# Another order of steps for the end of an attention, routing and expert kernel on one core

## The chip, the core and the metric

One core of a Trainium2 chip runs the whole program. The metric is the device time of one execution in microseconds (us). TensorE (PE) multiplies, with weight loads (PEld) beside it; VectorE (DVE), ScalarE (ACT) and GpSimd (POOL) do the elementwise work; SyncE (SP) issues most transfers. Each engine takes its instructions in the order of the program, and waits on semaphores where a result or a buffer comes from elsewhere.

## What is computed

The reference is an attention, a mixture of eight experts and a second multiplication stage, one behind the other:

```python
# attention: 4 x 12 heads, 448 positions, 64 wide; q and k normalised per row, then
scores = scale * (q_n @ k_n.T);  attn = softmax(scores);  x = attn @ v
# x becomes 1792 tokens x 768; experts: D = 768, E = 8, F = 1024
logits = x @ w_gate;  expert_idx = argmax(logits);  gate_w = its softmax probability
out[mask] = gate_w[mask] * (max(x[mask] @ w1[e], 0) @ w2[e])      # for each expert e
# second stage, on the experts' output x
h = (x @ w1) * (x @ w2) @ w3
return h @ w_out
```

## The kernel before

**Stages.** The attention runs over 12 groups of heads (about 0 to 325 us). Beside it the kernel multiplies w3 by w_out once (called W here; TensorE line 264), so that the second stage needs one product less. Then the tokens are routed, the experts run one after the other (from 372.9 us, lines 940, 964 and 968), and the second stage follows.

**The order.** Every piece of work is a generator that yields steps, each for one engine. `ORDER` is a string of 1388 two-character codes; `Flow.run` takes them in turn, sends the next step of that piece and pins the order on every engine. Nothing reorders steps afterwards. So the table alone sets in what order each engine, SP's queue among them, comes to its instructions.

**W.** A 64-bit piece of w3 or w_out is loaded (line 215, tile `w64`, two buffers), turned to 32-bit numbers by three DVE instructions (lines 205 to 207), split into a high and a low half (ACT lines 227 and 228, then POOL or DVE line 231, tile `w3r`), and for w3 turned by a DMA transpose (line 237, tile `w3t`). For the later pieces of the w3 rows from row block 4 on, second column half, there is one `w3r` buffer, so ACT line 228 of one such piece waits until the transpose of the one before has landed. A block of W, (row block f, column half n), is 24 matmuls of 128x384 into one PSUM buffer (`psw` or `pswl`), written out by ACT line 267, DVE line 269 and a store on SP (line 271). The three `s` PSUM buffers are shared by `pswl` blocks, by `psx` below and by the attention's scores before.

**Routing.** `route` (lines 590 to 632) compares the gate's sums `lacc` (line 525), finds each token's expert, and counts ranks by matmuls (`psr`, lines 614 to 618). `slots` (lines 660 to 676) makes masks `mk`, multiplies (`psi`, line 673) and writes the row numbers `ix0` of the first expert. `gather` fetches that expert's rows by three indirect transfers on POOL (line 723, tile `xr`), turns them with 36 small matmuls (line 742, `psx`) and copies them (DVE line 746, ACT line 748); expert 0 starts on TensorE behind that. `offsets` (lines 761 to 792) computes all positions `qi`; 14 indirect stores on POOL write the sorted list `md` (line 536), from which SP reads the next expert's rows (line 719).

**First expert's weights.** `prefetch` loads six pieces of w1 (line 698, ACT line 701, DVE line 703) and `prefetch2` eight of w2 (line 708, ACT line 711, DVE line 713) through three buffers `pf`.

Below, the functions that the diff touches.

Of the kernel before, what the change touches and what calls it, by code (L numbers as in the profile page):

```python
# [1462 lines left out]
```

## Time and profile before

| what | us |
|---|---|
| three runs: lowest, median, highest | 955.47, 956.5, 957.8 |
| the profiled execution | 957.36 |
| its span in the profile | 955.6 |

Busy shares over that span are PE 91%, DVE 66%, ACT 52% and POOL 33%. The mean hides that different engines bound different stretches: DVE is nearly full up to 140 us, PE from there to 325 us, and from 325 to 373 us neither is. A row of the timeline gives the start, the busy time, the engine, the line, the operation, what it writes and reads, the shape and the count; brackets hold the idle time of that engine just before and what ended it. In the table of windows PEclk is the granted clock of TensorE, 1.00 being 2.4 GHz and 0.50 being 1.2 GHz, and the DMA column is the mean busy share of the 16 DMA engines.

### The profile page before, as it was taken

Reading aid. Unit: us, or ns where it says so; the run is one execution under the profiler, and the core shown is the slowest. Engines: PE = TensorE matmul, PEld = TensorE weight load, DVE = VectorE, ACT = ScalarE, POOL = GpSimd, SP = SyncE. Lnnn points to the kernel's source line nnn. Section 1 sums busy time; section 2 is a strip of 40 time slices with the busy share of each in tenths; the row PEclk is TensorE's granted clock in tenths of the full one; section 3 lists DMA queues with packets and bytes.
Section 4 is the critical chain, followed back from the end, with each engine's and each line's share of the span. In section 5 each row is a group of like instructions: output and inputs, shape, how many; then the busy total and the mean of one; then the engine's idle time right before and its main releaser. Section 6 shows DMA issues by size and latency. Waiting matters only on the chain.

```text
span 955.6 us, 19437 instructions
## 1 busy us (share of the span) xinstructions
PE 871.3 (91%) x7766; PEld 587.8 (62%) x7766; DVE 626.2 (66%) x924; ACT 492.5 (52%) x770; POOL 315.5 (33%) x325
## 2 busy tenths in 40 slices
PE   0588999999999979899899999999889999999996
PEld 0255666666666645577688999975444445456664
DVE  6998998878998765247356787999964755120000
ACT  4877888888977443144356666654333323110000
POOL 6367567766733113410010101001443534131111
PEclk9989999999999997899899999999999999999999
DMA  7868799787589993386679899820322211111111
GB/s 186 184 140 198 179 191 195 142 177 156 110 219 216 223 253 83 130 231 183 207 245 285 246 296 299 266 84 2 109 67 66 67 45 50 50 67 50 50 50 50
DMA packets 200351, 144.44 MB, mean 151 GB/s; under 512 B 139376, under 2 KB 178832, under 8 KB 200256
## 3 DMA queue, kind: packets, MB, share of 16 engines
q1 hardware_dynamic: 197248, 131.39, 53.7%
q0 software_dynamic: 3008, 11.76, 3.6%
q8 instruction: 63, 1.03, 0.4%
q14 instruction: 32, 0.26, 0.1%
HBM read 103.52 MB, written 14.18 MB: 123 GB/s over the span
## 4 chain that ended last, share of the span: by engine, by line
PE 41%; DVE 7%; issue 2%; DMA 1%; ACT 1%; SPq 1%; POOLq 0%; ACTq 0%
PE psm L940 30%; PE pso L1433 11%; DVE m2w L1182 1%; DVE y32w L207 1%; DVE y32w L206 1%; DVE y32w L205 1%; DMA st<-in_moe_w_dram 1%; DVE c L1354 1%; DVE c L1344 0%; DVE b L1053 0%; SPq L957 0%; DVE c L1346 0%; ACT b L1050 0%; DMA sx<-in_moe_w_dram 0%; DVE y L1067 0%
## 5 line engine op out<-in xcount | busy, mean ns | idle before, releaser
L940 PE MATMUL psm<-b,m2w 128*128 128x512 f16 (+1 forms) x1008 | 193.8, 355 | 9.7 <-DVE m2w L1182 6.8
L940 PEld LDWEIGHTS <-m2w 128*128 128x128 f16 x1008 | 98.9, 98 | 104.3 <-DVE m2w L1182 8.0
L940 PEld LDWEIGHTS <-w1t 128*128 128x128 f16 x1152 | 110.8, 100 | 28.6 <-issue 9.9
L940 PE MATMUL psm<-ht,w2t 128*128 128x320 f16 (+7 forms) x1152 | 124.4, 270 | 0.0
L940 PEld LDWEIGHTS <-w2t 128*128 128x128 f16 x1152 | 109.2, 98 | 14.1
L940 PE MATMUL psm<-xte,w1t 128*128 128x288 f16 (+6 forms) x1008 | 107.2, 269 | 6.6 <-DMA sx<-in_moe_w_dram 4.7
L1433 PE MATMUL pso<-ww,ab 128*128 128x384 f16 x672 | 109.4, 326 | 0.0
L404 DVE TENSOR_REDUCE nm<-psm 128x2 f32<-128x896 f32 x84 | 88.6, 1083 | 9.8 <-PE psm L402 9.4
L1433 PEld LDWEIGHTS <-ab 128*128 128x128 f16 x672 | 65.8, 98 | 43.6
L1325 POOL TENSOR_TENSOR ab<-c,ab 128x384 f16<-128x384 f32 (+1 forms) x32 | 39.1, 1233 | 155.4 <-ACT ab L1324 152.1
L461 PE MATMUL po<-vf,e 128*128 128x65 f32 (+1 forms) x576 | 88.8, 272 | 1.5 <-issue 1.5
L402 PE MATMUL psm<-kt,qt 64*64 64x448 f16 x336 | 48.9, 390 | 40.6 <-DMA qt<-qf 27.9
L461 PEld LDWEIGHTS po<-vf,e 128*128 128x128 f32 (+1 forms) x576 | 69.9, 177 | 16.6 <-issue 13.3
L723 POOL DMA_INDIRECT xr<-xd,ix x19 | 20.8, 1097 | 177.6 <-DMA ix<-md 116.7
L1130 DVE SCALAR_TENSOR_TENSOR w1t<-st,w1t 128x1024 f16<-128x1024 f32 x42 | 50.8, 1223 | 35.7 <-ACT w1t L1124 34.4
L1437 DVE TENSOR_SCALAR ob<-pso,meta_s 128x384 f32<-128x384 f32 x14 | 8.7, 618 | 99.1 <-PE pso L1433 99.1
L431 PE MATMUL pss<-qt,kt 64*128 64x448 f16 (+1 forms) x576 | 67.3, 375 | 5.1 <-DVE e L446 4.0
L464 PE MATMUL po<-v,e 128*128 128x65 f16 (+1 forms) x480 | 63.8, 195 | 1.7 <-DVE lacc L525 1.7
L465 PE MATMUL po<-vl,e 128*128 128x64 f16 (+1 forms) x480 | 63.8, 194 | 0.0
L466 PE MATMUL po<-v,e 128*128 128x65 f16 (+1 forms) x480 | 63.0, 194 | 0.0
L1324 ACT ACTIVATE ab<-c 128x384 f16<-128x384 f32 (+1 forms) x32 | 18.2, 576 | 81.7 <-DVE c L1354 72.7
L1436 ACT ACTIVATE ob<-pso,meta_s 128x384 f32<-128x384 f32 x14 | 8.1, 580 | 98.8 <-PE pso L1433 98.8
(247 smaller groups left out, 1700.4 us busy)
## 6 DMA issues: line engine op xcount, KB each, us to landing
st<-in_moe_w_dram SPq DMA_DIRECT2D x42, 512.0 KB
st<-in_moe_w_dram SPq DMA_DIRECT2D x44, 384.0 KB
st<-in_moe_w_dram SPq DMA_DIRECT2D x48, 256.0 KB
w<-in_moe_w_dram SPq DMA_DIRECT2D x16, 512.0 KB
w<-in_moe_w_out_dram SPq DMA_DIRECT2D x16, 384.0 KB
xd<-rx SPq DMA_DIRECT2D x12, 448.0 KB
kf<-in_k_dram SPq DMA_DIRECT2D x24, 192.0 KB
qf<-in_q_dram SPq DMA_DIRECT2D x24, 192.0 KB
```

Of the source, the lines that this page charges most:

```text
L402: nc.tensor.matmul(ps[h, z, 0:S], lhsT=s["q"][0][h, c:c + 64], rhs=s["k"][0][h, S * j:S * j + S], start=True, stop=True)
L404: nc.vector.tensor_reduce(s["nm"][:, t], ps[:, :, 0:S], axis=AX.X, op=ALU.max, negate=True)
L431: nc.tensor.matmul(ps[o, h, 0:S], lhsT=l, rhs=rt[HD[h], S * j:S * j + S], start=a == 0, stop=a == 3)
L461: nc.tensor.matmul(ov[r, t, :], lhsT=e[0], rhs=vfs[i % 2][:, h, c, 0:D + 1], start=z == 0, stop=z == 3)
L464: nc.tensor.matmul(ov[r, t, :], lhsT=e[0], rhs=vh, start=z == 0, stop=False)
L465: nc.tensor.matmul(ov[r, t, 0:D], lhsT=e[0], rhs=s["vl"][:, h, c, :], start=False, stop=False)
L466: nc.tensor.matmul(ov[r, t, :], lhsT=e[1], rhs=vh, start=False, stop=z == 3)
L723: nc.gpsimd.indirect_dma_start(out=dst, out_offset=None, in_=xd, in_offset=bass.IndirectOffsetOnAxis(ap=ix[0:dst.shape[0], t:t + 1], axis=0))
L940: nc.tensor.matmul(ps, lhsT=x, rhs=y, start=first and j == 0, stop=last and j == n - 1, **kw)
L1130: nc.vector.scalar_tensor_tensor(t[:, 1], st, 32.0, t[:, 0], op0=ALU.mult, op1=ALU.subtract)
L1325: nc.gpsimd.tensor_tensor(ab[f][:, 1, cs], x, ab[f][:, 0, cs], op=ALU.subtract)
L1433: nc.tensor.matmul(pp[z], lhsT=ab[f][:, x, ts], rhs=ww[f][:, y, z * 384:(z + 1) * 384], start=f == 0 and x == 0 and y == 0, stop=f == 7 an ...
```

## The change

Only `ORDER` differs: four strings near its start (steps of 40 to 92 us) and its last 185 steps (from about 322 us up to the start of expert 0). No instruction is added or taken out: each engine has as many rows as before.

```diff
@@ -46,10 +46,10 @@
-    "0o0k0s1b0o0E200s1d0A0E0w0J1N0Acw1a0q0w1c1a0i1c0m1c0q1a0K0i0m221+0u0C0qcs0OcAcw22cs2Ycs0u261+0y0C0ucE2U1e0ycA1m24cw1e241q"
+    "0o0k0s1b0o0E200s1d0A0E0w0J1N0Acw1a0q0w1c1a0i1c0m1c0q1a0K0i0m221+0u0C0qcs0OcA22cs2Ycs0u261+0y0C0ucw2UcE1e0ycA1m24cw1e241q"
...
@@ -65,10 +65,10 @@
-    "d2doc+8ubfd6bgbgbgakc+dobgdoc+dod2dodudobibgbgdodwd6bsdybAdwbGd6dydubCdydwbGdwbEdubCbOdyd2dqbEbIdqdqdqbsbsbKdodqc4dqd6dq"
+    "d2do8ubfbgbgc+bgakc+dobgdodobic+bgdodudobgbsdobAbGdubCbEdududubsbsc4bsdudmdodudsdsdsc4c4d6d6bGbIc6c6c6d6dsdsdsdsdsdudwdw"
...
```

**The end of the attention.** The first place is on DVE, from `route`'s last instruction (line 609) to the masks `mk` and the row numbers `ix0`; `w1t` and `w2t` are weights of the first expert, `wsp` is a finished block of W, `w32` a piece of w3 on its way into W. Before:

```order
L609 CAST ohs_147<-ohf_148 128x56
L703 SCALAR_TENSOR_TENSOR w1t_5359<-pf_4962,w1t_5359 128x1024
L703 SCALAR_TENSOR_TENSOR w1t_5368<-pf_4411,w1t_5368 128x1024
L703 SCALAR_TENSOR_TENSOR w1t_5380<-pf_4304,w1t_5380 128x1024
L621 COPY rank_150<-psr_5410 128x56
L623 TENSOR_REDUCE sums_149<-ohf_148 128x8
L663 TENSOR_TENSOR fa_5427<-ohf_148,foh_153 128x56
L664 SCALAR_TENSOR_TENSOR fa_5427<-rank_150,fa_5427 128x56
L665 TENSOR_REDUCE fv_5428<-fa_5427 128x7
L668 TENSOR_SCALAR mk_5432<-slot_144,fv_5428 128x384 x7
L713 SCALAR_TENSOR_TENSOR w2t_5448<-pf2_5386,w2t_5448 128x768
L625 TENSOR_TENSOR ex_5324<-lg_5322,mx_5323 128x56
```

After:

```order
L609 CAST ohs_147<-ohf_148 128x56
L269 SCALAR_TENSOR_TENSOR wsp_5303<-psw_5204,wsp_5303 128x384
L621 COPY rank_150<-psr_5355 128x56
L623 TENSOR_REDUCE sums_149<-ohf_148 128x8
L663 TENSOR_TENSOR fa_5366<-ohf_148,foh_153 128x56
L664 SCALAR_TENSOR_TENSOR fa_5366<-rank_150,fa_5366 128x56
L665 TENSOR_REDUCE fv_5367<-fa_5366 128x7
L668 TENSOR_SCALAR mk_5371<-slot_144,fv_5367 128x384 x7
L625 TENSOR_TENSOR ex_5308<-lg_5306,mx_5307 128x56
L676 TENSOR_TENSOR ix0_146<-psi_5398,part_145 128x3
L205 TENSOR_SCALAR w32_5421<-w64_5087 128x512
L206 SCALAR_TENSOR_TENSOR w32_5421<-w64_5087,w32_5421 128x512
```

Three `w1t` pieces no longer stand between lines 609 and 621, and a `w2t` piece, a block `wsp` and a `w1t` piece no longer stand between lines 668 and 676; they, and two conversions of w3 that stood around the last `lacc` (line 525), come behind line 676.

Still on DVE, later, from the last copies of the turned rows (`xt0`) to the start of `offsets` (line 764). Before:

```order
L713 SCALAR_TENSOR_TENSOR w2t_5640<-pf2_5577,w2t_5640 128x768
L746 CAST xt0_5591<-psx_5676 128x640
L764 COPY own_155<-eidx_140 128x8
L765 COPY own_155<-psc_5620 128x8
L768 SCALAR_TENSOR_TENSOR key_5721<-own_155,rev_141 128x8
L769 SCALAR_TENSOR_TENSOR key_5721<-foh_153,key_5721 128x8
L770 TENSOR_TENSOR more_5722<-key_5721 128x64
```

After:

```order
L746 CAST xt0_5518<-psx_5581 128x640
L703 SCALAR_TENSOR_TENSOR w1t_5619<-pf_5615,w1t_5619 128x1024
L703 SCALAR_TENSOR_TENSOR w1t_5622<-pf_5617,w1t_5622 128x1024
L713 SCALAR_TENSOR_TENSOR w2t_5631<-pf2_5629,w2t_5631 128x768
L764 COPY own_155<-eidx_140 128x8
L765 COPY own_155<-psc_5588 128x8
L768 SCALAR_TENSOR_TENSOR key_5704<-own_155,rev_141 128x8
L769 SCALAR_TENSOR_TENSOR key_5704<-foh_153,key_5704 128x8
```

Two `w1t` pieces and a `w2t` piece now stand ahead of `offsets`; each waits for its own load.

The second place is SP's queue over the last two turnings of w3 (line 237) and the first expert's weight loads (lines 698 and 708). Before:

```order
L237 DMA_TRANSPOSE w3t_5443<-w3r_5319 128x8x128
L698 ISA
L698 DMA pf_5469<-in_moe_w1_dram 128x1024
L708 ISA
L708 DMA pf2_5505<-in_moe_w2_dram 128x768
L708 ISA
L708 DMA pf2_5527<-in_moe_w2_dram 128x768
L271 DMA wd_108<-wsp_5128 256x1x384
L271 DMA wd_108<-wsp_5493 256x1x384
L271 DMA wd_108<-wsp_5510 256x1x384
L237 DMA_TRANSPOSE w3t_5575<-w3r_5391 128x8x128
```

After:

```order
L237 DMA_TRANSPOSE w3t_5612<-w3r_5425 128x8x128
L271 DMA wd_108<-wsp_5511 256x1x384
L698 ISA
L698 DMA pf_5615<-in_moe_w1_dram 128x1024
L698 ISA
L698 DMA pf_5617<-in_moe_w1_dram 128x1024
L237 DMA_TRANSPOSE w3t_5627<-w3r_5508 128x8x128
L708 ISA
L708 DMA pf2_5629<-in_moe_w2_dram 128x768
L708 ISA
L708 DMA pf2_5634<-in_moe_w2_dram 128x768
```

The `w2` loads now go behind both turnings, and the last two `w1` loads (`pf_5615`, `pf_5617`) stand between the two.

On ACT, the same last two pieces of w3 (`w3r_5425`, `w3r_5508`, one buffer), in the order after:

```order
L227 ACTIVATE w32_5421<-w32_5421 128x512
L228 ACTIVATE w3r_5425<-w32_5421 128x512
L267 ACTIVATE wsp_5497<-psw_5388 128x384
L267 ACTIVATE wsp_5499<-pswl_5299 128x384
L227 ACTIVATE w32_5503<-w32_5503 128x512
L228 ACTIVATE w3r_5508<-w32_5503 128x512
L267 ACTIVATE wsp_5511<-pswl_5456 128x384
L701 ACTIVATE w1t_5513<-pf_5429 128x1024
L748 ACTIVATE xt0_5518<-psx_5519 128x640
```

Before, line 228 of the last piece came ahead of all `wsp` blocks here but one; now two blocks stand ahead of it and one, `wsp_5511`, behind it. On PE, `psr` and `psi` come some blocks of W sooner, and the six `psx` groups stand, with three or six W matmuls between each two, ahead of the 48 matmuls of W's last two blocks; before, five of the six stood among the first 24 of these 48. On POOL the three fetches `xr` now stand ahead of line 231 of the piece `w3r_5425`.

**The start.** The third place is on DVE at 80 to 92 us, where `nm` (line 404) is a maximum of the scores, `e` (line 446) the exponentials' low halves, and `w32` a piece of w_out. Before:

```order
L404 TENSOR_REDUCE nm_802<-psm_932 128x2
L446 TENSOR_TENSOR e_930<-pss_909,e_930 128x896
L205 TENSOR_SCALAR w32_988<-w64_846 128x384
L206 SCALAR_TENSOR_TENSOR w32_988<-w64_846,w32_988 128x384
L207 SCALAR_TENSOR_TENSOR w32_988<-w64_846,w32_988 128x384
L205 TENSOR_SCALAR w32_1005<-w64_783 128x384
L206 SCALAR_TENSOR_TENSOR w32_1005<-w64_783,w32_1005 128x384
L207 SCALAR_TENSOR_TENSOR w32_1005<-w64_783,w32_1005 128x384
L309 TENSOR_REDUCE ss_866<-kn_867 128x14
L404 TENSOR_REDUCE nm_802<-psm_983 128x2
```

After:

```order
L404 TENSOR_REDUCE nm_802<-psm_932 128x2
L446 TENSOR_TENSOR e_930<-pss_909,e_930 128x896
L404 TENSOR_REDUCE nm_802<-psm_983 128x2
L205 TENSOR_SCALAR w32_1055<-w64_846 128x384
L206 SCALAR_TENSOR_TENSOR w32_1055<-w64_846,w32_1055 128x384
L207 SCALAR_TENSOR_TENSOR w32_1055<-w64_846,w32_1055 128x384
L446 TENSOR_TENSOR e_1002<-pss_988,e_1002 128x896
L309 TENSOR_REDUCE ss_866<-kn_867 128x14
L205 TENSOR_SCALAR w32_1075<-w64_783 128x384
L206 SCALAR_TENSOR_TENSOR w32_1075<-w64_783,w32_1075 128x384
```

Line 404 of `psm_983` moves ahead of both conversions, and a line 446 ahead of the second. At 42 to 51 us one conversion likewise moves from ahead of two lines 309 and a line 446 to behind them.

## Rows read from the trace of the kernel before

**Rows 1.** The page, its part 2: busy tenths in 40 slices of 23.9 us.
```profile
PE   0588999999999979899899999999889999999996
...
DVE  6998998878998765247356787999964755120000
```

**Rows 2.** Windows: length; PE, PEld, DVE, ACT, POOL busy us; PEclk, DMA share, GB/s.
```profile
350.00:356.00 6.00, 1.03 (x6) 0.51 (x6) 2.67 (x8) 0.98 (x2) 0.00 (x0) 0.95 1.09 296
356.00:362.00 6.00, 5.78 (x27) 2.75 (x28) 1.69 (x2) 2.06 (x4) 0.00 (x0) 0.50 0.37 139
362.00:368.00 6.00, 6.00 (x29) 2.82 (x28) 2.47 (x4) 2.98 (x5) 0.00 (x0) 0.50 0.47 131
```

**Rows 3.** Timeline of PE, 332 to 373 us (start, busy, line, count, idle before).
```profile
332.41 0.49 PE L264 MATMUL psw<-woh,w3t 128*128 128x384 f16 x2
...
332.90 0.49 PE L264 MATMUL psw<-woh,w3t 128*128 128x384 f16 x2
...
352.24 0.23 PE L742 MATMUL psx<-ident,xr 128*128 128x128 f16 x1 [2.28 <-DMA xr<-xd,ix]
354.59 0.23 PE L742 MATMUL psx<-ident,xr 128*128 128x128 f16 x1 [2.12 <-DMA xr<-xd,ix]
355.43 0.72 PE L742 MATMUL psx<-ident,xr 64*128 64x64 f16 x4 [0.61 <-DMA xr<-xd,ix]
356.37 0.82 PE L264 MATMUL pswl<-woh,w3t 128*128 128x384 f16 x2 [0.22 <-DMA w3t<-w3r]
...
360.26 1.08 PE L742 MATMUL psx<-ident,xr 128*128 128x128 f16 x6
...
372.92 16.24 PE L940 MATMUL psm<-xt,w1t 128*128 128x320 f16 x117
```

**Rows 4.** Timeline of DVE, 329 to 373 us.
```profile
329.05 0.43 DVE L205 TENSOR_SCALAR w<-w 128x512 uint32<-128x512 uint32 x1 [3.08 <-DMA w<-in_moe_w_dram]
...
330.85 0.26 DVE L525 TENSOR_TENSOR lacc<-lacc,psl 128x112 f32<-128x112 f32 x1
...
334.03 3.49 DVE L703 SCALAR_TENSOR_TENSOR w1t<-pf,w1t 128x1024 f16<-128x1024 f32 x3
...
338.46 1.70 DVE L668 TENSOR_SCALAR mk<-slot,fv 128x384 f16<-128x384 f16 x7
...
344.46 0.15 DVE L676 TENSOR_TENSOR ix<-psi,part 128x3 uint32<-128x3 f32 x1
344.53 1.21 DVE L703 SCALAR_TENSOR_TENSOR w1t<-pf,w1t 128x1024 f16<-128x1024 f32 x1
...
372.50 0.17 DVE L792 CAST qi<-qf 128x14 uint32<-128x14 f32 x1
```

**Rows 5.** Timeline of POOL, from 344 us.
```profile
344.90 1.81 POOL L723 DMA_INDIRECT xr<-xd,ix  x1 [11.58 <-DVE ix L676]
```

**Rows 6.** Timeline of SP's queue, 325 to 374 us.
```profile
325.84 3.01 SPq L237 DMA_TRANSPOSE w3t<-w3r  x1
...
348.15 3.79 SPq L237 DMA_TRANSPOSE w3t<-w3r  x1
...
353.38 20.52 SPq L708 DMA_DIRECT2D pf<-in_moe_w_dram  x4
```

**Rows 7.** Timeline of ACT, 331 to 401 us.
```profile
331.46 0.63 ACT L228 ACTIVATE w3r<-w 128x512 f16<-128x512 f32 x1 [4.80 <-DMA w3t<-w3r]
...
400.50 1.06 ACT L1124 ACTIVATE w1t<-st 128x1024 f16<-128x1024 f32 x1 [0.46 <-DMA st<-in_moe_w_dram]
```

**Rows 8.** Timeline of DVE, 42 to 48 us.
```profile
42.25 0.56 DVE L207 SCALAR_TENSOR_TENSOR w<-w,w 128x384 uint32<-128x384 uint32 x1
...
45.44 2.31 DVE L207 SCALAR_TENSOR_TENSOR w<-w,w 128x384 uint32<-128x384 uint32 x1
```

**Rows 9.** Timeline of POOL, 44 to 48 us.
```profile
44.95 2.38 POOL L314 TENSOR_TENSOR kf<-kf,grow 128x896 f32<-128x896 f32 x1
```

**Rows 10.** Waits of PE, 20 to 140 us: us in total, times, longest.
```profile
PE psm L402 <- DVE e L446: 6.2, 2, 5.2
```

More of the change, by code (lines that the diff above doesn't have):

```diff
@@ L48 @@
     "1Wc8cc0+bm0Y040012c8ccc8ck10c8cg1K190610cc0602cc020a140M08140816ck0cckco0e0c0ccg0e0eclcg0c0Oco0ccs0eco0g1Mch0ecp160k0g1Y"
-    "0o0k0s1b0o0E200s1d0A0E0w0J1N0Acw1a0q0w1c1a0i1c0m1c0q1a0K0i0m221+0u0C0qcs0OcAcw22cs2Ycs0u261+0y0C0ucE2U1e0ycA1m24cw1e241q"
+    "0o0k0s1b0o0E200s1d0A0E0w0J1N0Acw1a0q0w1c1a0i1c0m1c0q1a0K0i0m221+0u0C0qcs0OcA22cs2Ycs0u261+0y0C0ucw2UcE1e0ycA1m24cw1e241q"
     "cIcA1m1i292+1q1y1i0Gcw281y1G1u0G0Q281o0Q1u2b282W0Q1o0G1CbkcE1k0Q2a1C0QcE2b2+1g1J0Q2W322a1g0Q1o0Q1A1k3QcA0Q1s30cI0Sbk1s0S"
-    "cQ310S3U2ccF1A1s370ScI2A2c2o0Q35cM0S2A360S3S2o0ScI2g0S2I37341w0S3Wbk1E2g0Q1w3W2k351E2s1O2k361O2s2E1O0S1E2K0S342e2wcM2m2e"
-    "0UcQ2m2i4Q1O3S2L1O2i1O2wcM384M2m2G1OcQ3+3c382q1O3Y1O2qcUcQca3c0U2u0W3Z2y2u2q432y3g0U2C3gcM4O3k1QcU2C1Q1Qcace1QcU1Q423o3k"
+    "cQ310S3U2ccF1A1s370ScI2A2c2o0Q35cM0S2A360S3S2o0ScI2g0S2I37341w0S3Wbk1E2g0Q1w3W2k351E2s1O2k361O2s2E1O0S1E2K0S342e2w2m2e0U"
+    "2m2i4Q1O2L1O2i1O2wcMcM384M2m3ScQ2G1O3+3c382q1O3YcQ1O2qcUcQca3c0U2u0W3Z2y2u2q432y3g0U2C3gcM4O3k1QcU2C1Q1Qcace1QcU1Q423o3k"
     "cUcY1Q1O1Q4S2C3A3w3Eca3o413a3w3e1Q3a1O1Q3i40cb2M3icY2Mca2M2M1Qd03s3G2M412M2McY2M43403i3s4S3D2Mce2OcY3m42ci4O1Q3u2Mce2O3m"
@@ L67 @@
     "aSdkdmaicOdmb2bGaidmagdmcOa+bcbcaib2dmcSaibcbccWakbcbcbcdmbccSd6dmbcdmdibebcc+cSbedmbecWbeamdmbebecXbedocWbedobedobdakbe"
-    "d2doc+8ubfd6bgbgbgakc+dobgdoc+dod2dodudobibgbgdodwd6bsdybAdwbGd6dydubCdydwbGdwbEdubCbOdyd2dqbEbIdqdqdqbsbsbKdodqc4dqd6dq"
-    "bOdwdqbOdudwbIbsdybMc4dqdwbKdwdqbIbSdudwc4dybKc6dsdydwbUc6dyd3bMdsduc6dsdybMdsbSdsdybsdsbSbsdmdsdqdwd2bWdyb+dsduduc6dAdA"
-    "dudsc6c6bUbudAdsduc6bUc6c6bYbWdAc6c6bWc0dAc6dAc6b+bYc0c6dCdCdCdAdCdAdCdCdAdCdCdCc6bub+bubQbubYbuc0budAbubQdCdCbQbudAdsbu"
-    "dubububububububu")
+    "d2do8ubfbgbgc+bgakc+dobgdodobic+bgdodudobgbsdobAbGdubCbEdududubsbsc4bsdudmdodudsdsdsc4c4d6d6bGbIc6c6c6d6dsdsdsdsdsdudwdw"
+    "dwdwdwdwdwdwdydydydydydsdudsdud2bCd2dwbIdwbEd3c6dyc6c6dyc6c6dyc6bsc6dqc6bIbsc6dqc6c6budqdqdqdqdqdqc6dsdud6dwbKbMbKbKbMdq"
+    "bMd2bObObObSbUdybSbWdAdAdAdAdAdAdCdCdCdAdCdAdCdCdAbUdCdCdCbWbudqdybSb+b+bubububudAbUbYbYbudCbWc0c0b+bQdydqbYc0bQdCbQbudA"
+    "bubububububububu")
 class Flow:
```

## The prediction

> **What bounds the kernel now.** I read the page's slices first, then windows of the stretch where no engine is full, then PE's timeline there, then followed each wait back through DVE, POOL, SP and ACT. From the fifth slice (96 us) to the fourteenth (334 us) PE shows a 9 throughout, while DVE is the fuller of the two in the four slices before; the fifteenth (334 to 358 us) is PE's only 7 [rows 1]. So nothing moved well inside PE's full stretch can be worth much. The stretch of interest lies between the end of the attention and the first expert's matmul at 372.92 [rows 3]. PE works only 1.03 of the 6 us from 350 to 356, and then runs two windows at a granted clock of 0.50, the 1.2 GHz level [rows 2]. The waits ahead of that are for the rows `xr` of the first expert: 2.28, 2.12 and 0.61 us, and behind them 0.22 for the turned last piece of w3 [rows 3].
>
> Why do `xr` come so late? POOL sends the fetch at 344.90, after 11.58 idle us, released by DVE's line 676 [rows 5]. That instruction is the end of a chain on DVE: `lacc` is complete at 330.85 + 0.26, because a conversion in front of it waited 3.08 us for its load; the masks start at 338.46, because three `w1t` pieces took 3.49 us on the way; and line 676 ends at 344.6, 4.4 us behind the masks' end [rows 4]. The row numbers themselves need far less.
>
> A second chain starts at `qi`, done at 372.67 [rows 4]. From it come the list `md`, the next expert's row list and loads, and the first converted weight of expert 1 at 400.50, where ACT waited only 0.46 us for the load [rows 7]. So this chain has no more than about half a microsecond of slack against SP's queue: what `qi` loses or gains, everything behind it does too. From 372.9 us on the order of both kernels is the same.
>
> **The end of the attention, part by part.** Nothing is added, so each term is a place in a queue.
>
> *Routing on DVE.* The conversion with its 3.08 us of waiting and its 1.8 us of work (329.05 to 330.85) leaves the way of `lacc`, and an earlier conversion does too: `lacc` some 5.2 us sooner, at about 325.6. The three `w1t` pieces go (3.49), against a `wsp` block that stays (0.55): masks start about 8.4 us sooner, at 330.1. Behind the masks, 4.4 us become the `psi` matmuls alone, about 1.7 us (estimated from the 4.4 us less the three pieces that stood there): 2.6 more. Sum: 11 us; line 676 ends at about 333.5, the fetches go out from 333.8. From fetch to use took 352.24 - 344.90 = 7.3 us for the first of the three tiles and 355.43 - 344.90 = 10.5 for the last [rows 3, 5], with the DMA engines full [rows 2]. So the rows are there at 341 to 344.4.
>
> *PE.* From the gate's matmuls at 326 to the first expert it has 171 matmuls of 128x384 left, three in 0.49 us (332.41 to 332.90 [rows 3]), so 0.163 each: 27.9 us. The 36 small `psx` matmuls cost 1.08 us a group at half clock [rows 3], so about 0.54 at full, 3 us in all; `psi`, `psr`, `psc` and `psl` about 3. Together 34 us: without any wait PE would be done at 360. Before it took until 372.9: 5.2 us of the four waits above, some 2 of smaller ones, and 6 for two windows of 6 us each at half clock [rows 2, 3], which adds up. So 13 us is the ceiling of this part.
>
> *The new waits.* The two conversions are moved behind line 676, so the last two pieces of w3 are turned later in the chain of W. They share one `w3r` buffer: ACT line 228 of the last one (`w3r_5508`) waits until the first has been turned. By my reckoning that turn is sent at 339.5 (conversion 1.8, two ACT steps 1.3 and POOL's line 231 1.2, the last behind three fetches). A turn took 331.46 - 325.84 = 5.6 us until ACT went on [rows 6, 7], and 356.37 - 348.15 = 8.2 us with the DMA engines full [rows 3, 6]. Queued behind that line 228 on ACT is line 267 of `wsp_5511`; its DVE half frees the PSUM buffer in which the first `psx` is wanted. PE runs out of other work at about 344.3. At 5.6 us the buffer is free at 346.8, a wait of 2.5; at 8.2 us at 349.4, a wait of 5.1. The second turn is then sent at 348.8 (351.4) and is wanted by PE at about 355 to 357: a further 0 to 2. I take the end near the first row, because the `w2` loads that filled the DMA engines then [rows 2] now stand behind both turns in SP's queue: 4 to 5 us of waits, no fall of the clock counted. Expert 0 starts at about 364.5: 8 us sooner. Both ends: 362.8 (10 sooner) and, with the long turn and a half clock again, 369 (4 sooner).
>
> *`qi`.* `offsets` took 4.7 us from line 764 to 792. Ahead of it on DVE now stand two `w1t` and one `w2t` piece, each behind its load, and these behind both turns on SP. Loads sent at 348 to 352 land some 4 to 6 us later, an estimate from the 5.6 us of a turn; conversion takes 1.21 us on DVE [rows 4]. So `offsets` begin at about 358 and `qi` is done at about 363: 9 to 10 us sooner, as much as PE. Both chains move together, so the 8 us pass through to the end. The `w2t` pieces go later, but expert 0 wants the first only after 144 matmuls of about 0.16 us, 23 us behind its start; that hides them.
>
> *DVE beside POOL.* A conversion now runs while POOL prepares the `xr` fetches. In this trace a `w1t` piece took 3.49 / 3 = 1.16 us with POOL idle and 1.21 us with the fetch of 344.90 beside it [rows 4, 5], so a cost of 0.05 an instruction, nothing, is entered. The Trainium skill, GPSIMD Engine Reference, section 1 (Specifications), says that GpSimd's SBUF interfaces are shared with VectorE, with contention for DVE instructions that have two SBUF inputs. By that alone the conversion and its turn would come later, and the wait at `psx` would grow by as much; these rows do not bear it out for fetches.
>
> **The start.** At 45.44 DVE's line 207 took 2.31 us where 0.56 is usual [rows 8]; POOL's line 314 ran beside it from 44.95 for 2.38 us [rows 9]. Behind this conversion on DVE stood the `e` for which PE waited 5.2 us [rows 10]. Put behind `e`, the conversion misses POOL's instruction: DVE saves 2.31 - 0.56 = 1.75 us of its own time, and `e` comes sooner by that and by the rest of the conversion. At 80 to 92 us POOL's work beside the conversions stays, but line 404 and `e` come sooner by one or two conversions of 1.5 to 3.3 us. Up to 96 us DVE is the fuller engine [rows 1], so what counts is mostly the DVE time saved: 1.75 for the first, 0 to 2 for the second. Behind that PE is full, so a gain made earlier stays. I take 2.5, with 0 and 4.5 as ends (4.5 if both reorderings count in full and PE's 5.2 us of waiting go down by more than the 1.75).
>
> **Sum.** 8 + 2.5 = 10.5 us off the profiled execution's 957.36 (1.8 of it outside the span, unchanged): 946.9. That execution lies 0.9 above the median, so on the median's scale 946.0.
>
> **Rivals.** *The clock falls once more.* PE's waits before `psx` and its six small groups come in the same way as at 350 to 356, after which the clock was 0.50. If the first turn takes 8.2 us, the wait is 5.1, about the 5.2 us at `e` early on. Half speed over half of the former 12 us costs 3, and the longer wait 2.6, of which 0.6 is taken back behind it: 5 us, so 951. The Trainium skill (TensorE: Matmul & The Clock Gate, section "HAM oscillation — how this bites in real kernels") says that waits for transfers between groups of matmuls let the clock fall again each time; before, the row of 356 to 362 agrees.
>
> *The early gain is lost* to another POOL instruction beside the moved conversions, or to the loads of w3, for which DVE waited 3.08 us at 329.05 [rows 4]: 948.5.
>
> *Nothing moves*, because the last turn of w3 still ends last: in the order it stands behind two more loads than before, and was sent at 348.15 [rows 6]. Should the chain of two turns through one buffer bring it no sooner than 356.4 and the clock be at half, PE would begin expert 0 at 371 to 373: 955 to 957.
>
> *Slower: `qi` behind the loads.* Four loads took SP 20.52 us from 353.38 on, since each waited for a buffer [rows 6]. If `pf_5617` and the `w2t` piece ahead of `offsets` are held up like that, so that the latter is converted after 368.2 (10 us later than I reckon), `qi` comes after 372.9 and each further microsecond costs one. At one further load spacing of 5 us: 957 + 5 - 2.5 = 959. Against it: those loads waited for conversions that here stand ahead of them.
>
> **How the numbers follow.** Forecast (941 to 949.5) 0.60; clock 0.17; early gain lost 0.10; nothing moves 0.07; slower 0.06. The range to 954 leaves out the last two and a little of the clock's case; its low end of 940 takes 10 and 4.5, with 2 for what hangs on the clock early. A measurement of this kernel tells 0.2%, 1.9 us, from no change: faster 0.90 (the first three and a third of the fourth), same 0.05 (the rest of the fourth), slower 0.05.
>
> **What would show it.** Right: the `xr` fetches at 331 to 335, first `psx` at 343 to 348, PE's expert 0 and `qi` both at 361 to 366, the stretch behind that the same length as before, and an interval from 100 us to the gate that starts 2 to 3 us sooner. Wrong: a granted clock of 0.50 between 345 and 360, `qi` later than expert 0's start by several us, or line 207 still above 2 us at the first moved place.

## The result, and the profile after

| | before | after |
|---|---|---|
| runs, lowest to highest, us | 955.47 to 957.8 | 944.51 to 947.79 |
| median, us | 956.97 | 945.6 |
| the profiled execution, us | 957.36 | 946.06 |
| its span in the profile, us | 955.6 | 944.0 |

The ratio is 0.9886, with a 95% interval of 0.9863 to 0.9908; by the medians it is 11.4 us sooner, and the forecast was 946.0. The number fits, but not as the sum that made it: the end of the attention gave far more than its 8 us, and the start, put down at 2.5 sooner, lost time.

The page of after, busy tenths in 40 slices (23.6 us each now), the answer to [rows 1]:

```profile
PE   0598999999999998998999999999899999999996
...
DVE  6999898888897876364556777999956644210000
```

PE's only 7, the fifteenth slice before, is gone: the fifteenth (330 to 354 us) is a 9 now. The 8 behind it lies in expert 0, of which more at the end. The windows over what was the slow stretch (length, then PE, PEld, DVE, ACT and POOL busy us; PEclk; DMA share; GB/s) answer [rows 2]:

```profile
344.00:350.00 6.00, 6.00 (x47) 3.59 (x46) 3.82 (x7) 2.71 (x6) 0.00 (x0) 1.00 0.94 281
350.00:356.00 6.00, 6.00 (x40) 3.62 (x41) 4.87 (x11) 3.79 (x6) 0.00 (x0) 1.00 0.60 172
356.00:362.00 6.00, 6.00 (x40) 3.76 (x39) 5.52 (x21) 2.40 (x5) 1.31 (x2) 1.00 0.33 94
```

PE is full and its clock is at 2.4 GHz in all three, where before one window held 1.03 us of work and the next two ran at 0.50. What made it so is read from the timelines. DVE, after, from the last attention output (line 486) to `qi`:

```profile
322.88 0.62 DVE L486 TENSOR_TENSOR x<-po,den 128x448 f32<-128x448 f32 x1
...
327.26 0.27 DVE L525 TENSOR_TENSOR lacc<-lacc,psl 128x112 f32<-128x112 f32 x1 [0.70 <-PE psl L523]
...
331.49 1.70 DVE L668 TENSOR_SCALAR mk<-slot,fv 128x384 f16<-128x384 f16 x7
...
333.81 0.16 DVE L676 TENSOR_TENSOR ix<-psi,part 128x3 uint32<-128x3 f32 x1 [0.49 <-PE psi L673]
...
354.49 0.96 DVE L713 SCALAR_TENSOR_TENSOR w2t<-pf,w2t 128x768 f16<-128x768 f32 x1 [0.99 <-ACT w2t L711]
355.37 0.17 DVE L764 COPY own<-eidx 128x8 f32<-128x8 f32 x1
...
359.92 0.17 DVE L792 CAST qi<-qf 128x14 uint32<-128x14 f32 x1
```

POOL, SP and ACT after, the answers to [rows 5 to 7] (first fetch; the two last turns of w3; line 228 of the last two pieces):

```profile
334.26 1.09 POOL L723 DMA_INDIRECT xr<-xd,ix  x1 [5.79 <-DVE ix L676]
```

```profile
339.41 1.80 SPq L237 DMA_TRANSPOSE w3t<-w3r  x1
...
344.98 1.26 SPq L237 DMA_TRANSPOSE w3t<-w3r  x1
```

```profile
336.50 0.63 ACT L228 ACTIVATE w3r<-w 128x512 f16<-128x512 f32 x1
...
341.48 0.63 ACT L228 ACTIVATE w3r<-w 128x512 f16<-128x512 f32 x1
```

PE after, the answer to [rows 3]: the first turned rows, expert 0's first matmul, expert 1's first:

```profile
342.90 0.28 PE L742 MATMUL psx<-ident,xr 128*128 128x128 f16 x2
343.63 0.55 PE L742 MATMUL psx<-ident,xr 64*128 64x64 f16 x4 [0.46 <-DMA xr<-xd,ix]
...
360.83 2.61 PE L940 MATMUL psm<-xt,w1t 128*128 128x320 f16 x18
...
406.75 8.49 PE L940 MATMUL psm<-xte,w1t 128*128 128x288 f16 x68
```

The four waits of 5.2 us in all ahead of and among the `psx` groups [rows 3] have become one of 0.46. The last instruction of the attention itself, though, came sooner before. DVE, before:

```profile
321.12 0.62 DVE L486 TENSOR_TENSOR x<-po,den 128x448 f32<-128x448 f32 x1
```

So the 11.6 us of span are made up like this: the attention ends 1.8 later (322.88 against 321.12); from there to expert 0 it is 13.9 shorter (37.95 for 51.80); expert 0 is 0.3 shorter; what lies behind is 0.8 longer.

### The profile page after: what moved, and what is told of

The parts are those of the page before. It is cut to its first block, busy times and chain, and to the rows that moved or that the text cites. A ratio compares the mean times of both kernels' runs of the same rounds, so it can differ in the third digit from the quotient of the medians.

```text
span 944.0 us, 19445 instructions
## 1 busy us (share of the span) xinstructions
PE 868.6 (92%) x7766; PEld 586.2 (62%) x7766; DVE 625.8 (66%) x924; ACT 492.9 (52%) x770; POOL 313.8 (33%) x325
## 3 DMA queue, kind: packets, MB, share of 16 engines
q8 instruction: 63, 1.03, 0.4%
## 4 chain that ended last, share of the span: by engine, by line
PE 42%; DVE 7%; issue 2%; ACT 1%; POOLq 0%; ACTq 0%
PE psm L940 31%; PE pso L1433 11%; DVE m2w L1182 1%; DVE y32w L207 1%; DVE y32w L206 1%; DVE y32w L205 1%; DVE b L1053 1%; DVE c L1354 1%; DVE c L1344 0%; DVE c L1346 0%; ACT b L1050 0%; DVE w1t L1130 0%; DVE y L1067 0%; DVE y32w L1165 0%; ACT c L1340 0%
## 5 line engine op out<-in xcount | busy, mean ns | idle before, releaser
L940 PEld LDWEIGHTS <-w2t 128*128 128x128 f16 x1152 | 109.0, 98 | 13.9
L402 PE MATMUL psm<-kt,qt 64*64 64x448 f16 x336 | 49.6, 395 | 37.7 <-DMA qt<-qf 27.6
L461 PEld LDWEIGHTS po<-vf,e 128*128 128x128 f32 (+1 forms) x576 | 70.3, 178 | 17.2 <-issue 13.9
L1130 DVE SCALAR_TENSOR_TENSOR w1t<-st,w1t 128x1024 f16<-128x1024 f32 x42 | 50.8, 1223 | 37.2 <-ACT w1t L1124 36.5
```

The lines of the kernel that those rows point to most:

```text
L402: nc.tensor.matmul(ps[h, z, 0:S], lhsT=s["q"][0][h, c:c + 64], rhs=s["k"][0][h, S * j:S * j + S], start=True, stop=True)
L461: nc.tensor.matmul(ov[r, t, :], lhsT=e[0], rhs=vfs[i % 2][:, h, c, 0:D + 1], start=z == 0, stop=z == 3)
L940: nc.tensor.matmul(ps, lhsT=x, rhs=y, start=first and j == 0, stop=last and j == n - 1, **kw)
L1130: nc.vector.scalar_tensor_tensor(t[:, 1], st, 32.0, t[:, 0], op0=ALU.mult, op1=ALU.subtract)
```

## The experiments

The runs share two yardsticks: the time against the kernel before on the same chip, and lengths inside the one profiled execution, which tell more, since single runs of one kernel differ by 5 to 16 us there. Lengths are in us from the start of the last line 486 (the end of the attention); "at 1.2 GHz" is the time that PE's clock was granted at 0.50 between there and expert 0; the last column runs from expert 0's first matmul to expert 1's, with any wait for expert 1's rows at its end.

| kernel | fetch | first psx | qi | expert 0 | at 1.2 GHz | expert 1 | expert 0's length |
|---|---|---|---|---|---|---|---|
| before | 23.8 | 31.1 | 51.4 | 51.8 | 13.7 | 98.0 | 46.2 |
| early_only | 23.5 | 31.2 | 48.8 | 48.3 | 6.8 | 91.0 | 42.6 |
| after | 11.4 | 20.0 | 37.0 | 38.0 | 0 | 83.9 | 45.9 |
| after_again | 11.4 | 20.0 | 38.1 | 39.0 | 0 | 81.8 | 42.9 |
| tail_only | 11.4 | 20.0 | 40.4 | 41.3 | 6.8 | 83.7 | 42.5 |
| first_and_tail | 11.4 | 20.0 | 37.7 | 38.6 | 0 | 80.9 | 42.3 |
| second_later_and_tail | 11.4 | 20.0 | 37.5 | 38.4 | 0 | 79.7 | 41.3 |
| second_later_again | 11.4 | 20.0 | 37.2 | 38.2 | 0 | 80.5 | 42.3 |
| second_later_qi_sooner | 11.4 | 20.0 | 32.7 | 37.8 | 0 | 81.9 | 44.0 |
| fetch_late | 14.7 | 26.3 | 42.8 | 43.7 | 6.8 | 91.5 | 47.8 |
| fetch_behind_half | 15.6 | 21.8 | 42.4 | 43.3 | 3.4 | 85.4 | 42.0 |
| turns_late | 11.4 | 20.0 | 36.9 | 45.0 | 3.4 | 93.1 | 48.1 |
| qi_late | 11.4 | 20.0 | 44.8 | 40.6 | 0 | 88.7 | 48.1 |

From expert 1's start to the last matmul every one of them takes 527 to 531 us: nothing that the change moves reaches further.

### The two halves of the change, each alone

`tail_only` is the kernel before with the new last 185 steps; `early_only` is the kernel before with the new strings near the start.

```diff
 tail_only: ORDER, from the end of the attention
-    "d2doc+8ubfd6bgbgbgakc+dobgdoc+dod2dodudobibgbgdodwd6bsdybAdwbGd6dydubCdydwbGdwbEdubCbOdyd2dqbEbIdqdqdqbsbsbKdodqc4dqd6dq"
+    "d2do8ubfbgbgc+bgakc+dobgdodobic+bgdodudobgbsdobAbGdubCbEdududubsbsc4bsdudmdodudsdsdsc4c4d6d6bGbIc6c6c6d6dsdsdsdsdsdudwdw"
...
 early_only: ORDER, 40 to 51 us (and the two strings of 80 to 92 us)
-    "...E200s1d0A0E0w0J1N0Acw1a0q0w1c1a0i1c0m1c0q1a0K0i0m221+0u0C0qcs0OcAcw22cs2Ycs0u261+0y0C0ucE2U1e0ycA1m24cw1e241q"
+    "...E200s1d0A0E0w0J1N0Acw1a0q0w1c1a0i1c0m1c0q1a0K0i0m221+0u0C0qcs0OcA22cs2Ycs0u261+0y0C0ucw2UcE1e0ycA1m24cw1e241q"
```

> The order of before up to the middle of the attention, and the changed order from there to the end: only the end is changed. Theory A (the profile after: the end alone gives everything, the attention ends 1.6 us later because of the start): expert 0 begins 13.5 us sooner than before, 943.5 us. Theory B (as predicted: 8 us from the end, 2.5 from the start): 949.

> The changed order of the start (the places at 42 to 51 and 80 to 92 us), the order of before from there on. Theory A (the second place costs what the first gains, and a little drifts away behind it): the last gate sum 1.5 us later, 958.5 us. Theory B (as predicted): 2.5 us sooner, 954.5.

Measured: `tail_only` 943.77, ratio 0.9846 (0.9802 to 0.9889); `early_only` 956.51, ratio 0.9997 (0.9967 to 1.0027). The end of the attention carries all of the gain that can be measured, and the start carries none that can; the interval of `early_only`, 2.9 us to either side, holds both of the theories for it. `tail_only` also ran into the first rival of the prediction, in this execution: PE waited at the last of the rows, and then the clock fell. PE and the window behind, `tail_only`:

```profile
342.86 0.55 PE L742 MATMUL psx<-ident,xr 64*128 64x64 f16 x4 [1.15 <-DMA xr<-xd,ix]
```

```profile
346.00:352.00 6.00, 6.00 (x31) 2.90 (x32) 2.62 (x7) 2.76 (x5) 0.00 (x0) 0.52 0.78 251
```

It cost about 3 us, 41.3 to expert 0 against 38.0 to 39.0 in the five executions of the same end whose clock held: the 3 that the prediction had put on the half speed itself.

### Which of the two early places

`first_and_tail` keeps the new order at 42 to 51 us but the old one at 80 to 92; `second_later_and_tail` is the changed kernel with the first conversion of the second place behind line 309 as well. Both with the new end.

```diff
 second_later_and_tail: DVE at 80 to 92 us, against the changed kernel
 L404 TENSOR_REDUCE nm
-L205 TENSOR_SCALAR w32_1055
-L206 SCALAR_TENSOR_TENSOR w32_1055
-L207 SCALAR_TENSOR_TENSOR w32_1055
 L446 TENSOR_TENSOR e
 L309 TENSOR_REDUCE ss
+L205 TENSOR_SCALAR w32_1069
+L206 SCALAR_TENSOR_TENSOR w32_1069
+L207 SCALAR_TENSOR_TENSOR w32_1069
```

> The first early place (42 to 51 us) and the end changed, the second place (80 to 92 us) as before. Theory A (the first place gains 2.3 us that stay, the second place loses them): 941 us, line 404 of the third group 2.3 us sooner than before, the granted clock at 88 to 96 us as before. Theory B (the stretch behind, 95 to 140 us, takes back what comes early, whatever the second place does): 943.5, as with the end alone.

> As the changed kernel, but both conversions of the second place stand behind line 309, where POOL was idle. Theory A (the second place loses because its first conversion runs beside POOL's lines 386, 416 and 314, 5.1 us for 1.5, and PE then waits at the slower clock): the conversions take 1.5 us each, DVE saves 3.6 us, 941 us. Theory B (the loss is that line 404 and the sums behind it are put later): no sooner than the changed kernel, 945.

> The changed kernel once more, on the chip of the next two. Theory A (the gain is the one measured first): 0.9886 of before within half a per cent. From the last but one gate sum to the first matmul of expert 0: 36 us where no half clock falls in, up to 39.5 where it does (48 in the kernel before, of which 13.7 us at half clock).

> Both conversions of the second early place behind line 309, and the changed end, beside the changed kernel on the same chip. Theory A (the conversions beside POOL cost 2 us at 80 to 92 us, and that stays): 2 us less than the changed kernel in the same call. Theory B (what the later stretch does with its granted clock outweighs it): no difference that this chip's spread lets show, within 0.4%.

Measured: `first_and_tail` 941.61, ratio 0.9852 (0.9807 to 0.9898); `second_later_and_tail` 941.05, 0.9832 (0.9782 to 0.9883); and on another chip the changed kernel itself (`after_again`) 944.84, 0.9876 (0.9832 to 0.992) beside `second_later_again` 942.82, 0.9873 (0.9825 to 0.992). The times lie where the theories A had them, but the intervals hold the theories B too: by time alone neither beats the changed kernel. The traces do tell the places apart, because every kernel that was run with a new start gives one more execution of it. Line 404 comes in twelve groups of seven, one for each group of the attention, and the shift of a group's last `nm` against before, less the shift of the group ahead of the place, is what the place gave (us, minus is sooner):

| executions | first place, group 0 to 1 | second place, group 1 to 3 |
|---|---|---|
| both old (tail_only) | 0.0 | 0.0 |
| both new (after, after_again, early_only, fetch_late, turns_late, qi_late, fetch_behind_half) | -2.1, -1.2, -0.9, +0.5, +0.8, -2.3, +0.4 | +3.0, +2.0, +1.7, +2.5, +2.4, +3.0, +2.6 |
| first new, second old (first_and_tail) | -1.2 | -1.1 |
| first new, second put later (the three second_later kernels) | -2.3, -2.3, -2.3 | +1.1, +0.1, +0.2 |

In all seven the second place loses 1.7 to 3.0 us, and in none of the others does it lose over 1.1. The rows show why. DVE and POOL of the changed kernel there:

```profile
80.41 1.72 DVE L205 TENSOR_SCALAR w<-w 128x384 uint32<-128x384 uint32 x1
82.16 1.07 DVE L206 SCALAR_TENSOR_TENSOR w<-w,w 128x384 uint32<-128x384 uint32 x1
83.27 2.32 DVE L207 SCALAR_TENSOR_TENSOR w<-w,w 128x384 uint32<-128x384 uint32 x1
```

```profile
79.79 2.12 POOL L386 TENSOR_TENSOR vl<-vf,v 128x1024 f16<-128x1024 f32 x1 [0.76 <-ACT v L383]
81.87 0.94 POOL L416 TENSOR_TENSOR dg<-eye,nm 128x384 f16<-128x384 f16 x1
82.78 2.39 POOL L314 TENSOR_TENSOR kf<-kf,grow 128x896 f32<-128x896 f32 x1
```

The same conversion put behind line 309, DVE of `second_later_again`:

```profile
84.14 0.50 DVE L205 TENSOR_SCALAR w<-w 128x384 uint32<-128x384 uint32 x1
84.67 0.56 DVE L206 SCALAR_TENSOR_TENSOR w<-w,w 128x384 uint32<-128x384 uint32 x1
85.26 0.56 DVE L207 SCALAR_TENSOR_TENSOR w<-w,w 128x384 uint32<-128x384 uint32 x1
```

DVE of the kernel before, the same place:

```profile
82.23 2.37 DVE L207 SCALAR_TENSOR_TENSOR w<-w,w 128x384 uint32<-128x384 uint32 x1
```

`nm` moved ahead releases POOL's line 416 sooner, and line 314 follows it at once. The conversion stands beside three POOL instructions in a row and takes 5.1 us. Before, line 386 alone stood beside it, and only its line 207 was slowed; behind line 309 all three take 1.6. At the first place the opposite holds, as forecast. DVE after:

```profile
45.53 1.08 DVE L446 TENSOR_TENSOR e<-pss,e 128x896 f16<-128x896 f32 x1
...
47.50 0.56 DVE L207 SCALAR_TENSOR_TENSOR w<-w,w 128x384 uint32<-128x384 uint32 x1
```

Line 207, 2.31 us before [rows 8] beside line 314 [rows 9], takes 0.56, and PE's wait for this `e` is shorter. PE after:

```profile
46.66 2.45 PE L402 MATMUL psm<-kt,qt 64*64 64x448 f16 x12 [3.01 <-DVE e L446]
```

The gain reaches PE in eight of the eleven executions that have this place new; in the other three (fetch_late, turns_late, fetch_behind_half) the clock stays at half speed and `nm` waits for PE instead (2.61 us for `psm`, at 61.91, in `turns_late`). A window of `turns_late`:

```profile
54.00:60.00 6.00, 6.00 (x38) 3.60 (x35) 5.23 (x7) 4.29 (x5) 3.40 (x2) 0.50 0.56 112
```

In the changed kernel's own execution the same window has 0.83.

### What the fetch is worth

Two ways to hold it back. `fetch_late` puts three `w1t` pieces back on DVE between lines 609 and 621. `fetch_behind_half` moves one thing only: on POOL the three fetches go behind line 231 of the piece `w3r_5425`.

```diff
 fetch_late: DVE, against the changed kernel
 L609 CAST ohs
 L269 SCALAR_TENSOR_TENSOR wsp
+L703 SCALAR_TENSOR_TENSOR w1t x3
 L621 COPY rank
...
 fetch_behind_half: POOL, against the changed kernel
+L231 TENSOR_TENSOR w3r<-w32_5421
 L723 DMA_INDIRECT xr x3
-L231 TENSOR_TENSOR w3r<-w32_5421
```

> The changed kernel, but the first three w1t pieces stand again between lines 609 and 621 on DVE, as before the change: row numbers and fetches some 3.5 us later (from 334.3 to 337.8). Theory A (the fetched rows are what PE waits for, and nothing stands in for them in its fixed order): the first psx 3 to 3.5 us later, a gap of that length on PE, expert 0 3.5 us later, and more if the granted clock falls; 949 to 952 us. Theory B (the turns of w3 end last, the rows have room): expert 0 within 1 us of the changed kernel's, 946.

> The changed kernel, but on POOL the three fetches of the rows stand behind line 231 of the piece of w3 in front of them, nothing else is moved: fetches 4.2 us later against line 676. Theory A (the rows are what PE waits for ahead of psx): a gap of 4 us on PE at the first psx groups, expert 0 4 us later against the last but one gate sum, 40 us instead of 36, and up to 43 if the clock falls. Theory B (PE reaches psx late for another reason, the wait of 0.46 us there is all): 37 us at most.

Measured: `fetch_late` 954.35, ratio 0.9978 (0.9947 to 1.0008); `fetch_behind_half` 951.12, 0.9949 (0.9924 to 0.9975). POOL's and PE's rows of `fetch_behind_half`:

```profile
344.69 1.33 POOL L723 DMA_INDIRECT xr<-xd,ix  x1 [0.16 <-issue]
```

```profile
350.87 0.23 PE L742 MATMUL psx<-ident,xr 128*128 128x128 f16 x1 [1.66 <-DMA xr<-xd,ix]
...
353.14 0.23 PE L742 MATMUL psx<-ident,xr 128*128 128x128 f16 x1 [2.04 <-DMA xr<-xd,ix]
...
353.81 0.58 PE L742 MATMUL psx<-ident,xr 64*128 64x64 f16 x4 [0.44 <-DMA xr<-xd,ix]
```

The fetch leaves 4.3 us later; PE waits 4.1 in the very three places of [rows 3], some half speed follows, and expert 0 starts 5.4 later than after. That is the mechanism of the prediction by itself: the fetch sets `psx`, and a wait there costs its length and some more for the clock. The time agrees: the interval lies wholly above that of `after_again`, on the same chip. `fetch_late` costs expert 0 about the same (5.7), and more in time than the 949 to 952 of its theory A, but by another way than I meant. PE of `fetch_late`:

```profile
340.15 1.94 PE L673 MATMUL psi<-ids,mk 128*128 128x1 f16 x21 [2.31 <-DVE mk L668]
```

PE stopped 2.31 at the masks, ahead of the fetch, ran at half speed behind that, and so reached `psx` after the rows were there. The window behind:

```profile
342.00:348.00 6.00, 6.00 (x24) 2.85 (x22) 2.41 (x5) 1.84 (x4) 4.15 (x4) 0.51 0.51 152
```

In this order PE has a fixed place for `psi`; the pieces on DVE delay PE itself and not the rows alone.

### Do the last two pieces share a buffer?

The prediction's new wait rested on one `w3r` buffer for both. `turns_late` sends the first of the last two turns behind the last two `w1` loads, and the second behind three `w2` loads.

```diff
 SP, against the changed kernel
-L237 DMA_TRANSPOSE w3t (first of the last two)
 L271 DMA wd<-wsp
 L698 DMA pf (two w1 loads)
-L237 DMA_TRANSPOSE w3t (second)
+L237 DMA_TRANSPOSE w3t (first)
 L708 DMA pf (three w2 loads)
+L237 DMA_TRANSPOSE w3t (second)
```

> The changed kernel, but on SP the first of the last two turns of w3 stands behind the last two w1 loads, and the second behind three w2 loads. Theory A (the prediction: both pieces share one buffer, so a late first turn holds ACT's line 228 of the second, and with it the PSUM buffer of the first psx): the first psx 3 to 6 us later. Theory B (the pieces have a buffer each, and only the last blocks of W want the turns): the first psx where it is in the changed kernel, and a wait of 3 to 6 us ahead of the last blocks of W; 949 to 952 us in both.

Measured: 954.43, ratio 0.9981 (0.9955 to 1.0008). ACT, SP and PE of `turns_late`:

```profile
343.97 0.63 ACT L228 ACTIVATE w3r<-w 128x512 f16<-128x512 f32 x1
```

```profile
347.45 1.27 SPq L237 DMA_TRANSPOSE w3t<-w3r  x1
...
356.24 1.24 SPq L237 DMA_TRANSPOSE w3t<-w3r  x1
```

```profile
361.19 0.82 PE L264 MATMUL pswl<-woh,w3t 128*128 128x384 f16 x2 [5.65 <-DMA w3t<-w3r]
```

Line 228 of the last piece wrote its `w3r` 3.5 us ahead of the first piece's turn. So they don't share a buffer, and my term for it was wrong. The kernel's source says why: line 225 takes the buffer of a late piece by its column half, and by the order table the last two pieces are the two halves of row block 7. The trace of before had it already. ACT and SP before:

```profile
335.48 0.63 ACT L228 ACTIVATE w3r<-w 128x512 f16<-128x512 f32 x1
```

```profile
338.55 1.70 SPq L237 DMA_TRANSPOSE w3t<-w3r  x1
```

Line 228 of the last piece ran at 335.48, without idle time before it, 3.1 us ahead of the turn of the piece written at 331.46. The wait of 4.80 there [rows 7] is between two pieces of the same half. In `turns_late` the first `psx` stood where it stands after (20.0), with a wait of 0.31; the late turn is met only at W's last blocks, where PE waited 5.65 and expert 0 came 7 us later, as theory B had it. The time is above its 949 to 952; this execution also has one of the two longest expert 0 of the table (48.1). The turns have little room, but at the other end of the stretch than I had said.

### What `qi` is worth

`qi_late` puts three `w2t` pieces and W's last four `wsp` blocks ahead of `offsets` on DVE. `second_later_qi_sooner` is second_later_and_tail with `offsets` ahead of the two `w1t` pieces and the `w2t` piece.

```diff
 qi_late: DVE, against the changed kernel
 L713 SCALAR_TENSOR_TENSOR w2t
+L269 SCALAR_TENSOR_TENSOR wsp x4, L713 SCALAR_TENSOR_TENSOR w2t x3, mixed
 L764 COPY own ... L792 CAST qi
-L269 SCALAR_TENSOR_TENSOR wsp x4, L713 SCALAR_TENSOR_TENSOR w2t x3, mixed
...
 second_later_qi_sooner: DVE, against second_later_and_tail
-L703 SCALAR_TENSOR_TENSOR w1t x2
-L713 SCALAR_TENSOR_TENSOR w2t
 L764 COPY own ... L792 CAST qi
+L703 SCALAR_TENSOR_TENSOR w1t x2
+L713 SCALAR_TENSOR_TENSOR w2t
```

> The changed kernel, but three w2t pieces and the last four blocks of W stand ahead of the offsets on DVE: qi some 7 us later, expert 0 where it is. Theory A (the prediction: from qi on a chain without slack leads to expert 1; in the runs whose expert 0 had no stall, expert 1 began 43 us behind qi): expert 1 begins at 410 or later, 4 to 7 us later than in the changed kernel; 950 to 953 us. Theory B (expert 0 on PE sets expert 1's start, the chain has room): no change, 946.

> As the kernel with both conversions behind line 309, and the offsets on DVE ahead of the last two w1t pieces and the first w2t piece: qi 4 us sooner against the start of expert 0, those pieces 4.7 us later. Theory A (the chain from qi sets expert 1's start wherever expert 0 runs without a stall): expert 1 2 to 3 us sooner than without this move, 939 us. Theory B (expert 0 wants those pieces as soon): it starts 1 to 3 us later and the gain is gone, 941.

Measured: `qi_late` 949.49, ratio 0.9932 (0.9897 to 0.9966); `second_later_qi_sooner` 944.41, 0.9861 (0.9815 to 0.9907). `qi` came 7.8 later than after and 4.8 sooner than in second_later_and_tail; expert 1 came 4.8 later than after, and no sooner than in the other second_later kernels (81.9 against 79.7 and 80.5). The time of `second_later_qi_sooner` lies above both theories, 939 and 941, though its interval holds the second. Neither is a pure test, as the rows show. PE of `qi_late`, and the row of PE's waits, 355 to 410 us, in `second_later_qi_sooner` (us in total, times, longest):

```profile
363.11 3.13 PE L940 MATMUL psm<-xt,w1t 128*128 128x320 f16 x13 [2.45 <-DVE own L765]
```

```profile
PE psm L940 <- DVE wsp L269: 3.2, 1, 3.2
```

In the one, expert 0's first matmul waited 2.45 for `offsets`' own read of the counts in PSUM; in the other, 3.2 for the `wsp` block that was put behind them. PE's work and the chain from `qi` end at nearly the same time: when expert 0 runs undisturbed, expert 1 waits for its own rows, as here in `second_later_again`:

```profile
400.02 8.16 PE L940 MATMUL psm<-xte,w1t 128*128 128x288 f16 x54 [2.59 <-DMA xte<-xr]
```

All seven executions whose expert 0 takes 41.3 to 42.9 us end it with this wait, of 1.6 to 3.4 us, and in them expert 1 begins 42.1 to 43.8 us behind `qi`: there the chain from `qi` sets expert 1, as the prediction had it. Where expert 0 is longer (45.9 in after), there is no such wait, as the row at 406.75 above shows, and PE sets it. So `qi` is one of two limits that stand some microseconds apart, not one that passes on all of its shift.

## Why the prediction was right, and where its sum was not

**What bounds, and where the gain lies: right.** The fetch was released by line 676, and all that stood on DVE's way to it was work that it did not need. Counted from the end of the attention, against [rows 4], `lacc` came 5.4 us sooner (5.2 forecast), the masks 8.7 (8.4), line 676 12.4 (11). The prediction's times go by the end of the attention before; after, it lies 1.8 us later. With those 1.8 taken off, the fetch left at 332.5 (333.8 forecast). PE without waits would be done at 360, I had said; taken so, expert 0 began at 359.1.

**The new waits: wrong.** The step that failed is "They share one `w3r` buffer", with 4 to 5 us of waits at its end. `turns_late` shows two buffers; after shows line 228 of the last piece at 341.48, with no idle time before it, and the first `psx` at 342.90 (341.1 with the 1.8 taken off), not 346.8; the first turn left at 339.41 (337.6, against 339.5), and the second at 344.98 (343.2), 5.6 ahead of the 348.8 that the shared buffer would have allowed. So the end of the attention did not give 8 but 13.9 us in this pair, a little over the 13 that I had called its ceiling. Idle time of PE between the end of the attention and expert 0 fell from 7.5 us in all to 0.6: 4.8 of it are the waits at the rows and the turn (5.2 before, 0.46 after), the rest smaller ones. The remaining 6.9 are, to 0.1, half of the 13.7 us at half speed, gone. In `tail_only`, with 6.8 us at half speed left, it was 10.5.

**The clock: right as a rival, and not settled by the wait alone.** `tail_only` waited 1.15 us at the third tile of rows, and its next full window ran at 0.52. In `after_again` PE waited longer at the same place, and the window behind it stayed at full speed (in `first_and_tail`, with 1.12 us there, too):

```profile
345.02 0.55 PE L742 MATMUL psx<-ident,xr 64*128 64x64 f16 x4 [1.30 <-DMA xr<-xd,ix]
```

```profile
348.00:354.00 6.00, 6.00 (x45) 3.60 (x44) 4.73 (x9) 3.41 (x5) 0.00 (x0) 1.00 0.83 242
```

The Trainium skill (TensorE: Matmul & The Clock Gate, section "HAM oscillation — how this bites in real kernels") has the clock fall again at each wait for a transfer between groups of matmuls, in a kernel whose waits were of some 3 to 5 us. Before, with 5.0 us of waits for the rows in three pieces, the trace agrees; in `tail_only` the clock fell behind a wait far shorter than those, and in `after_again` it did not.

**The start: right at the first place, wrong sign at the second.** The first place saved the 1.75 us of DVE time at line 207 and 0.59 more that I had not seen: line 206 of the same conversion took 1.15 us before, beside POOL's line 231 at 44.00, and 0.56 after. PE's wait there fell from 5.2 [rows 10] to 3.0. For the second I had entered 0 to 2 us of gain, "POOL's work beside the conversions stays". That is the step: it does not stay, since the same reordering releases POOL sooner, and 1.7 to 3.0 us were lost in seven executions of seven. The attention ended 1.8 us later where 2.5 sooner was forecast; the rival "the early gain is lost to another POOL instruction beside the moved conversions" came true, at a chance of 0.10.

**DVE beside POOL's fetches: right.** The fetch had been entered as free for a conversion beside it; after, a `w1t` piece took 1.24 us at 335.68, beside the second fetch. What slowed conversions was POOL's own tensor work. The Trainium skill (GPSIMD Engine Reference, section 1, Specifications) tells of contention for DVE instructions with two SBUF inputs or in a 2-port mode. The rows of lines 206 and 207 agree (0.56 alone; 1.07 and 2.32 beside POOL). Line 205, which reads one tile only, was slowed as well: 0.35 alone, 1.72 here; whether it ran in such a mode no run here shows.

**`qi` and PE move together: right** (14.4 and 13.9 us sooner, counted from the attention's end). The rival that ended slower, `qi` held up behind loads, had little to it here: the `w2t` piece ahead of `offsets` waited 0.99 us at 354.49, and `offsets` began at 355.37, not the 358 I had reckoned. That what `qi` gains or loses is gained or lost behind it holds only where expert 0 runs undisturbed, as shown above. Nothing hung on the 23 us that hide the `w2t` pieces, but by [rows 3] expert 0's matmuls take 0.14 us each (16.24 for 117) and not 0.16, which makes it 20.

**The sum.** The end gave 5.9 more than its term and the start 4.3 less; the errors nearly cancel, and that the measured 945.6 lies so near the forecast of 946.0 is luck in that respect. That the end alone ran at 943.77, where the sum would have made it 949, says the same.

**What stays open.** Expert 0 takes 41.3 to 42.9 us in seven of these executions and 44 to 48 in the six others. One of the six, `second_later_qi_sooner`, has the 3.2 us for `wsp` shown above. In the five others, before, after, fetch_late, turns_late and qi_late, PE is idle for some 3 to 5 us without a releaser in the profile. After:

```profile
374.00:380.00 6.00, 2.39 (x14) 0.94 (x12) 2.17 (x4) 2.13 (x5) 3.74 (x4) 1.00 0.43 99
```

PE works 2.39 of 6 us, while POOL issues the transfers of `md`. No run here tells why it comes in some executions only. It is as large as what the early places could give. Nor was every part of the new end taken back by itself: on PE `psr`, `psi` and `psx` come ahead of blocks of W, and no run has the old order there with the new one elsewhere. What the runs show is that a fetch 4.3 us later, with all else new, costs 5.4 of the 13.9 us, and the three `w1t` pieces 5.7.

## What to carry to other kernels

Work back from a wait to the engine that issues the transfer, and list what stands ahead of that issue and isn't needed by it: a new order built round that gave all of the gain that could be measured, with no instruction added or removed. A reordering that releases a second engine sooner also moves that engine's work: look up what will then run beside the moved instructions, not what ran beside them before. And a buffer that two tiles are said to share should be read from the trace (did the writer ever wait for the reader?) before a wait is priced on it.

## What the hardware showed that was not expected

One and the same gap is followed by very different stretches at half speed. Every execution has an idle 1.54 us on PE between 110 and 116 us, with no releaser in the profile. Within 1 us of it a stretch at half speed begins that lasts 13.65 us in four executions and 3.41 in five; in the four others none begins within 10 us of it. PE before, the window from 120 us before, and that of `early_only`, where the gap of 1.54 ends at 113.93:

```profile
112.73 0.82 PE L461 MATMUL po<-vf,e 128*128 128x65 f32 x4 [1.54 <-issue]
```

```profile
120.00:128.00 8.00, 7.06 (x79) 3.54 (x78) 7.42 (x14) 6.77 (x11) 6.88 (x4) 1.00 0.72 171
```

```profile
120.00:128.00 8.00, 8.00 (x68) 6.00 (x70) 3.23 (x7) 2.89 (x7) 5.41 (x3) 0.55 0.81 193
```

The clock is back at full speed in the window from 120 us in the one, and at 0.55 in the other, though PE is never idle there. Between the fourth and the fifth group of the attention that is worth 4.4 to 4.5 us, in four of the thirteen executions (`early_only`, `fetch_late`, `fetch_behind_half`, `second_later_qi_sooner`); in the nine others the two groups stay within 0.6 us of their distance before. The runs of one kernel scatter by this much and more (before: 951 to 965 us in all but two of the 63 runs that stand beside the experiments). How much of that scatter this stretch makes isn't shown, since only the profiled executions have a trace; but with such steps about, an early gain of 2 us can be read from the groups in the trace, and not from the times.
